# Two of four blocks of x move from the start-up into the loop's first ten steps, and wo is read in eight parts

## The chip, the core and the metric

The kernel runs on one core of a Trainium2 chip. The metric is device time in microseconds, the median of several executions. The core has five engines with a program each: PE (matrix products), DVE (vector), ACT (activations), POOL (a second vector engine) and SP, which here only issues transfers. Transfers issued by SP go through one queue; the data moves on the core's 16 DMA engines.

## The reference

One transformer block with modulated normalisation: attention of 2048 rows over a cache of 2048 keys for each of 32 heads, then a mixing layer and an MLP. Cut to what the change touches:

```python
mod = (_silu(c) @ w_mod).reshape(c.shape[0], 6, 1, -1)     # c: 640 values, w_mod: 640 x 3840
sa, ca, ga, sb, cb, gb = (mod[:, 0].copy(), ...)
h = _layernorm(x, axis=-1) * (1 + ca) + sa                 # x: 2048 x 640
q = (h @ wq).reshape(B, Sq, H, Dh)                         # 32 heads of 128
p = _softmax(einsum(q, k_cache) * Dh ** -0.5)              # per head 2048 x 2048
x = x + ga * (concat of heads(p @ v_cache) @ wo)           # wo: 4096 x 640
...                                                        # then the second half, with sb, cb, gb
```

## The kernel before

Every instruction is written by hand into one list per engine. The class `Prog` keeps those lists; `G.op` and `G.dma` append to them and derive the waits from keys that an operation reads (`r`) and writes (`w`). Each engine runs its list in order, so the order of the Python calls is the order of the work.

**Start-up (lines 380 to 483).** The 2048 rows of x come in four blocks of 512 (`load_x`), and `w_mod` in two parts: the first two of its six pieces as columns (`wmod`), the other four as rows (`wmodr`). For each block, `stats` takes means and variances on DVE (L423, L426) with the root on ACT (L428), `normed` normalises on DVE (L432, L435), and `to_hT` turns five 128-wide pieces on PE (L446) and applies scale and shift, alternating between ACT (L450) and DVE (L455). `cols` (L412) computes the scale and the shift from silu(c) on PE. `q_head0` makes the queries of head 0 for that block (`q_piece`, L294, and `q_evac`, L301). This is done for all four blocks, apart from the last block's queries, before the loop begins. `c` is read as 640 elements of two bytes by a transfer on SP's queue.

**The loop (lines 596 to 668)** has one step s for each head and each tile of 128 rows: 32 x 16 = 512 steps, and 14 more to drain. In step s PE makes the scores (`qk`, L344 and L15, two halves of 1024), DVE scales them into `negS` with a running minimum (L642, one pass for each half), POOL joins the two minima (L647), and ACT takes the exponential into a slot of `ring` (L650). `negS` holds three steps. The exponentials must be turned before they meet V. For 27 of every 32 steps that is a DMA transposition of three steps together (a trio; `transpose`, L279, on SP's queue, issued after the exponential of its last step). For the other five, PE turns them (`t_piece`, L311) and ACT copies them back (`t_evac`, L318). Ten steps later (`PVD`) PE multiplies them with V (`pv`, L358), and after every second step ACT copies the result to `Of` (L629). POOL divides by the sum and writes it to a scratch tensor in DRAM. The queries of the next head are made on the way (`q_piece` on PE, `q_evac` on ACT).

`ring` has 20 slots, given out by `take` as six windows of three (`WIN`) and two single slots (`ONE`). In the start-up the same memory holds x, `wmod`, `wmodr` and small tables; `wo` has memory of its own and is read by one transfer at the end of the start-up's issues (L393).

In steps 0 to 2 `mod_rows` (L492) multiplies silu(c) with the rows of `w_mod` on PE, spread over all partitions by `s_bc`, and ACT copies the result to `mod_bc` (L495), which the kernel first reads after the loop. The last block's queries of head 0 are made in step 0.

**SP's queue in the loop.** Besides the transpositions it holds the next head's K (`load_k`, at tile 2 of a head), the head after next's `wq` (`load_wq`, at tile 6) and the next head's V (`load_v`, at tile 11). After the loop, `a_pe` (L584) multiplies the heads' results with `wo`, and the mixing layer and the MLP follow.

## Time and profile before

| | us |
|---|---|
| median of 3 runs (1540.65 to 1544.33) | 1543.39 |
| the profiled execution | 1540.59 |
| its span, first to last instruction | 1538.4 |
| end of the last transfer of x (block 3) | 15.7 |
| first pass of DVE over scores (L642) | 35.2 |
| first exponential (L650) | 38.8 |
| exponential of step 10 | 65.4 |
| end of the last exponential, step 511 | 1222.0 |
| landing of `wo` (issued at 31.9) | 48.6 |

The page of the profile gives, for each engine, its busy time and share of the span. A line of the timeline has start, duration, engine, source line, operation, the tiles written and read and their shapes; in brackets stands how long the engine was idle before it and what released it. A line of a wait view has the engine and line that waited, what it waited for, the time in total, how often, and the longest. Where a view of one source line is narrowed to one transfer, "took" is the time that SP needed to issue it and "DMA to landing" the time from the start of the issue until its data was there.

The granted clock of PE is 0.997 over the span, and 0.90 over the first 34.5 us.

### The profile page before, as it was taken

To read this page: it belongs to the slowest core of one execution; us is meant where nothing else is said; L and a number is where in the kernel's file an instruction comes from. 1 tells how busy PE (TensorE), PEld (TensorE's weight loads), DVE (VectorE), ACT (ScalarE), POOL (GpSimd) and SP (SyncE) were. 2 spreads that over 40 slices of the span, in tenths; PEclk is the share of its full clock that TensorE was granted. 3 is DMA by queue.
4 is the path that set the end of the run, shared out by engine and by line. 5 is a ranking of instruction groups with operands and counts; after the bars stand their busy time and mean duration, and the time that the engine had idled before them with its cause. 6 is when DMAs were issued, how large, how long until landed. Compare 5 with 4: busy or idle time off the path is not lost.

```text
span 1538.4 us, 32439 instructions
## 1 busy us (share of the span) xinstructions
PE 1474.0 (96%) x13447; PEld 920.1 (60%) x12663; DVE 1372.8 (89%) x2431; ACT 1253.7 (81%) x1177; POOL 622.6 (40%) x1397
## 2 busy tenths in 40 slices
PE   5899999999999999999999999999999999999999
PEld 3366666666666666566666666666666655554545
DVE  7999999999999999999999999999999746668425
ACT  4999999999999999999999999999999800034230
POOL 0144444444444444444444444444444433323000
PEclk9999999999999999999999999999999999999999
DMA  9999999999999999999999999999999997724100
GB/s 288 239 235 238 240 246 229 255 233 248 232 248 242 247 235 233 232 245 246 238 234 244 238 232 258 229 247 239 245 236 244 236 259 165 150 63 126 35 22 35
DMA packets 1153110, 330.29 MB, mean 215 GB/s; under 512 B 1133568, under 2 KB 1146944, under 8 KB 1152960
## 3 DMA queue, kind: packets, MB, share of 16 engines
q1 hardware_dynamic: 1144480, 307.09, 100.8%
q0 software_dynamic: 6144, 16.79, 3.5%
q10 hardware_dynamic: 2336, 4.34, 0.8%
q8 instruction: 103, 1.69, 0.4%
q14 instruction: 47, 0.39, 0.1%
HBM read 43.48 MB, written 19.40 MB: 41 GB/s over the span
## 4 chain that ended last, share of the span: by engine, by line
ACT 71%; PE 20%; DVE 5%; DMA 2%; issue 1%; POOL 0%; ACTq 0%
ACT ring L650 59%; PE Sps L584 9%; ACT ring L318 5%; ACT Of L629 4%; ACT kv L301 4%; PE Sps L887 4%; DVE negS L642 3%; DMA ring<-ring 2%; PE Oaug L838 2%; PE QPp L838 2%; PE Sps L823 1%; DVE ring L423 1%; PE Oaug L760 1%; PE QPp L760 1%; DVE ring L435 0%
## 5 line engine op out<-in xcount | busy, mean ns | idle before, releaser
L642 DVE TENSOR_SCALAR_CACHE_REDUCE negS<-Sps 128x1024 f32<-128x1024 f32 x1024 | 1173.3, 1222 | 12.8 <-PE Sps L15 12.8
L650 ACT ACTIVATE ring<-negS,small 128x2048 bf16<-128x2048 f32 x512 | 1078.9, 2185 | 4.9 <-POOL small L647 4.7
L358 PEld LDWEIGHTS PTp<-kv,ring 128*128 128x128 bf16 x8192 | 557.4, 98 | 288.3 <-issue 48.5
L358 PE MATMUL PTp<-kv,ring 128*128 128x129 bf16 x8192 | 644.8, 220 | 11.9 <-DMA ring<-ring 10.9
L15 PE MATMUL Sps<-kv 128*128 128x512 bf16 x1009 | 383.1, 380 | 9.8 <-DVE negS L642 6.1
L344 PE MATMUL Sps<-kv 128*128 128x512 bf16 x956 | 370.4, 387 | 17.1 <-DVE negS L642 4.9
L647 POOL TENSOR_SCALAR small<-small 128x1 f32<-128x1 f32 x512 | 145.9, 285 | 591.3 <-DVE negS L642 591.2
L506 POOL TENSOR_SCALAR On<-Of,small 128x128 bf16<-128x128 f32 x512 | 189.8, 371 | 13.0
L344 PEld LDWEIGHTS Sps<-kv 128*128 128x128 bf16 x1024 | 98.1, 96 | 152.4 <-DVE negS L642 113.8
L629 ACT COPY Of<-PTp 128x259 f32<-128x259 f32 x256 | 139.2, 544 | 15.5 <-PE PTp L358 15.5
L499 POOL TENSOR_TENSOR small<-Of,small 128x4 f32<-128x4 f32 x128 | 133.1, 1040 | 11.8 <-ACT Of L629 11.7
L513 POOL DMA_DIRECT2D o_scratch<-On x128 | 103.4, 808 | 40.8 <-POOL On L506 37.2
L294 PE MATMUL Oaug<-hTx,kv 128*128 128x512 bf16 x258 | 97.8, 384 | 3.2 <-DVE hTx L455 3.2
L294 PE MATMUL QPp<-hTx,kv 128*128 128x512 bf16 x259 | 97.5, 381 | 2.3 <-ACT hTx L450 1.6
L768 ACT ACT_TABLE_LOAD x1 | 1.3, 1283 | 111.8 <-POOL hTx L786 111.8
L642 DVE DVE_READ_ACCUMULATOR negS<-Sps 128x1 f32 x1024 | 87.5, 85 | 0.0
L681 POOL TENSOR_SCALAR negS<-negS 128x1 f32<-128x1 f32 x48 | 24.4, 509 | 123.3 <-DVE negS L690 123.3
L584 PE MATMUL Sps<-wo,negS 128*128 128x128 bf16 (+1 forms) x503 | 69.9, 298 | 0.5
L584 PE MATMUL Sps<-wo,hTx 128*128 128x512 bf16 (+1 forms) x502 | 69.3, 297 | 0.5
L695 DVE TENSOR_TENSOR ring<-Sps,mod_bc 128x640 f32<-128x640 f32 x16 | 13.1, 821 | 60.6 <-PE Sps L584 60.6
L891 DVE TENSOR_TENSOR ring<-Sps,ring 128x640 f32<-128x640 f32 x15 | 12.4, 824 | 59.5 <-PE Sps L887 59.5
L311 PE MATMUL Oaug<-identf,ring 128*128 128x128 f32 x320 | 62.1, 276 | 1.3 <-ACT ring L650 1.3
(88 smaller groups left out, 1071.5 us busy)
## 6 DMA issues: line engine op xcount, KB each, us to landing
kv<-in_A_v_cache_dram SPq DMA_DIRECT2D x32, 512.0 KB, 5.3
o_scratch<-On POOLq DMA_DIRECT2D x128, 128.0 KB, 5.3
kv<-in_A_wq_dram SPq DMA_DIRECT2D x32, 160.0 KB, 3.4
wo<-in_A_wo_dram SPq DMA_DIRECT2D x1, 5120.0 KB, 16.7
ring<-in_A_x_dram SPq DMA_DIRECT2D x5, 640.0 KB, 6.6
ring<-in_w_mod_dram SPq DMA_DIRECT2D x1, 3200.0 KB, 14.5
out_dram<-wo SPq DMA_DIRECT2D x15, 160.0 KB, 1.7
ring<-ring SPq DMA_TRANSPOSE x144, 9.6
```

The costliest lines, as they stand in the source:

```text
L15: return t.add_instruction(mybir.InstMatmult(name=t.bass.get_next_instruction_name(), ins=[t.lower_ap(rhs), t.lower_ap(lhsT)], outs=[t.low ...
L294: G.op("tensor", lambda t: t.matmul(JB[jb], wq[:, hb, q, :], hT[:, q, cc * 512:(cc + 1) * 512], start=(q == 0), stop=(q == KT - 1)), r=[(" ...
L344: ins = (t.matmul if c2 == 0 else partial(same_weights, t))(Sps[:, col:col + 512], QT[:, hb, j * 128:(j + 1) * 128], KTs[:, hb, col:col + ...
L358: ins = t.matmul(ob[:, 0:129], pt, Vaug[:, hb, kt, 0:129], start=(kt == 0), stop=(kt == NKT - 1))
L499: G.op("gpsimd", lambda g: g.tensor_tensor(out=rl[:, 4 * b:4 * b + 4], in0=Of[:].rearrange("p a z d -> p (a z) d")[:, 4 * b:4 * b + 4, 128 ...
L506: G.op("gpsimd", lambda g: g.tensor_scalar(out=On[:, b, z, :], in0=Of[:, 2 * b + z // 2, z % 2, 0:128], scalar1=rl[:, 4 * b + z:4 * b + z ...
L513: G.dma("gpsimd", lambda e: e.dma_start(o_scr[jj // 2:jj // 2 + 2, :, hh].rearrange("a p z d -> p a (z d)"), On[:, b].rearrange("p (a z) d ...
L584: ins = t.matmul(YB[b][:, c0:c0 + cw], OTj[pr % 2][:, 2 * hh + z, :], wo[:, hh, c0:c0 + cw], start=(hh == 0), stop=(hh == H - 1))
L629: G.op("scalar", lambda a, p=p: a.copy(Of[:, p % 4].rearrange("p z d -> p (z d)")[:, 0:259], PO[:, (p % 2) * 512:(p % 2) * 512 + 259]), r= ...
L642: G.op("vector", lambda v, half=half, dst=dst, src=src, r8=r8: v.tensor_scalar(out=dst, in0=src, scalar1=-SCALE, scalar2=None, op0=ALU.mul ...
L647: G.op("gpsimd", lambda g, r8=r8: g.tensor_scalar(out=nm[:, r8:r8 + 1], in0=nm0[:, r8:r8 + 1], scalar1=nm1[:, r8:r8 + 1], scalar2=None, op ...
L650: G.op("scalar", lambda a, s=s, r8=r8: a.activation(ring[:, PSL[s], :], negS[:, s % 3, :], ACT.Exp, bias=nm[:, r8:r8 + 1], scale=-1.0), r= ...
```

## The change

The start-up does block 0 completely, and takes block 1 up to its normalised rows. The rest is written into two tables: `EARLY[s]` runs in step s after PE's work of that step, and `LATE[s]` after its exponential. Blocks 1, 2 and 3 are turned, rescaled and projected for head 0 in steps 0 to 9; the statistics of half of block 2 and all of block 3, and both normalisings, stand in steps 0 to 4, with the root on POOL in place of ACT. All rescaling of these blocks is on ACT. The five `mod_rows` move from steps 0 to 2 to steps 3 to 7 and use other banks. An exponential of one column (`dume`) in the start-up loads ACT's table before the loop.

The order of SP's issues is new: the columns of `w_mod` right after x's block 0, the first `wq` and K ahead of x's blocks 2 and 3, the rows of `w_mod` ahead of V. `c` is read as five rows of 128 on ACT's queue and turned by a matmul with `ident`. `wmod` and x lie in slots 0 to 9 of `ring`; all the other start-up buffers lie in `wo`'s memory (key `WOR`). `wo` is read in eight parts of four heads' rows (640 KB) at steps 29, 93, 157, 221, 285, 349, 413 and 461. `load_wq(2)` moves from step 6 to step 11.

```diff
-                WIN = [0, 3, 6, 11, 14, 17]
-                ONE = [9, 10]
+                WIN = [0, 3, 6, 10, 13, 16]
+                ONE = [19, 9]
...
-                free_at = dict(zip(WIN, (0, 1, 3, 2, 4, 5)))
+                free_at = dict(zip(WIN, (0, 2, 5, 4, 1, 3)))
...
+                WOP = H // 8
+
+                def load_wo(i):
+                    G.dma("sync", lambda e: e.dma_start(
+                        wo[:, i * WOP:(i + 1) * WOP], A_wo[i * WOP * 128:(i + 1) * WOP * 128, :].rearrange("(h p) n -> p h n", p=128)),
+                        ("wo", i), w=(["WOR"] if i == 0 else []) + [("wop", i)] + (["wo", "woz", "wo4"] if i == 7 else []))
+                G.dma("scalar", lambda e: e.dma_start(c_row, c[0].rearrange("(kt p) -> kt p", p=128)), "c", r=WOR, w=["c"])
                 load_x(0)
-                G.dma("sync", load_c, "c", w=["c"])
+                load_mod(0, wmod, 0, 2 * D)
                 load_x(1)
-                load_mod(0, wmod, 0, 2 * D)
+                load_wq(0)
+                load_k(0)
                 for cc in range(2, NQC):
                     load_x(cc)
-                load_wq(0)
-                load_k(0)
-                load_v(0)
-                load_mod(1, wmodr, 2 * D, 6 * D)
                 if H > 1:
                     load_wq(1)
+                load_mod(1, wmodr, 2 * D, 6 * D)
+                load_v(0)
+                if H > 1:
                     load_k(1)
-                G.dma("sync", lambda e: e.dma_start(wo[:], A_wo.rearrange("(h p) n -> p h n", p=128)), "wo", w=["wo", "woz", "wo4"])
...
+                G.op("tensor", lambda t: t.matmul(JB[0][:, 0:KT], c_row, ident[0:KT, 0:KT], start=True, stop=True),
+                     r=["c", "ident"] + WOR, w=[("J", 0)])
+                G.op("scalar", lambda a: a.activation(s_col, JB[0][:, 0:KT], ACT.Silu), r=[("J", 0)] + WOR, w=["scol"])
...
+                def root(cc, on_act):
+                    c4 = slice(4 * cc, 4 * cc + 4)
+                    if on_act:
+                        G.op("scalar", lambda a: a.activation(sd[:, c4], mv[:, c4, 1], ACT.Sqrt, bias=float(EPS)),
...
+                    else:
+                        G.op("gpsimd", lambda g: g.tensor_scalar(out=sd[:, c4], in0=mv[:, c4, 1], scalar1=float(EPS),
...
+                        G.op("gpsimd", lambda g: g.tensor_tensor(out=rstd[:, c4], in0=sd[:, c4], in1=mh4, op=ALU.pow),
...
+                def to_hT(cc, ks, banks, on_v=()):
+                    for k, b in zip(ks, banks):
+                        turn(cc, k, b)
+                    for k, b in zip(ks, banks):
+                        modul(cc, k, b, k in on_v)
...
+                stats(0, 0, 4)
+                root(0, True)
+                normed(0)
+                stats(1, 0, 2)
+                G.op("tensor", cols, r=["scol", ("wm", 0)] + WMK + WOR, w=[("J", 1)])
...
+                to_hT(0, range(KT), range(KT), (1, 3))
+                stats(1, 2, 4)
+                q_head0(0)
+                root(1, True)
+                G.op("scalar", lambda a: a.activation(dume, mh4[:, 0:1], ACT.Exp), r=["mh4"] + WOR, w=["dume"])
+                normed(1)
+                stats(2, 0, 2)
+                bcast()
+                EARLY = {0: [(to_hT, 1, (0, 1, 2), (4, 5, 7), ())],
+                         1: [(to_hT, 1, (3, 4), (4, 5), ())],
+                         2: [(to_hT, 2, (0, 1), (4, 5), ()), (q_head0, 1)],
+                         3: [(to_hT, 2, (2, 3), (4, 5), ()), (mod_rows, 0, 2)],
+                         4: [(to_hT, 2, (4,), (4,), ()), (mod_rows, 1, 1), (mod_rows, 2, 2), (q_head0, 2)],
+                         5: [(to_hT, 3, (0, 1), (4, 5), ()), (mod_rows, 3, 2)],
+                         6: [(to_hT, 3, (2, 3), (4, 5), ())],
+                         7: [(to_hT, 3, (4,), (4,), ()), (mod_rows, 4, 1)],
+                         8: [(mod_end,)],
+                         9: [(q_head0, 3)]}
+                LATE = {0: [(stats, 2, 2, 4), (root, 2, False)],
+                        1: [(normed, 2)],
+                        2: [(stats, 3, 0, 2)],
+                        3: [(stats, 3, 2, 4), (root, 3, False)],
+                        4: [(normed, 3)]}
+                WOAT = {29: [0], 93: [1], 157: [2], 221: [3], 285: [4], 349: [5], 413: [6], 461: [7]}
...
-                    G.op("tensor", f, r=[("OT", pr % 2, i) for i in parts] + [("OTa", pr % 2)] + ["wo", "woz", "wo4"], w=[("S", b)])
+                    G.op("tensor", f, r=[("OT", pr % 2, i) for i in parts] + [("OTa", pr % 2)] + ["wo", "woz", "wo4"] + [("wop", i) for i in range(8)], w=[("S", b)])
...
-                    if s <= 2:
-                        for i in ((0,), (1, 2), range(3, len(MROW)))[s]:
-                            mod_rows(i)
...
-                        if s == 0 and half == 1:
-                            q_head0(NQC - 1)
...
                     for fn, x, y in evacs:
                         fn(x, y)
+                    for fn, *args in EARLY.get(s, ()):
+                        fn(*args)
...
                         G.op("scalar", lambda a, s=s, r8=r8: a.activation(
                             ring[:, PSL[s], :], negS[:, s % 3, :], ACT.Exp, bias=nm[:, r8:r8 + 1], scale=-1.0),
                             r=[("negS", s % 3), ("nm", r8)], w=slot(PSL[s]))
+                        for fn, *args in LATE.get(s, ()):
+                            fn(*args)
                         if s in last_of:
                             transpose(last_of[s])
...
-                        if j == 6 and h + 2 < H:
+                        if j == (6 if h else 11) and h + 2 < H:
                             load_wq(h + 2)
+                        for i in WOAT.get(s, ()):
+                            load_wo(i)
```

## The prediction

> **What bounds the kernel now.** I read the page first, for the engine that the end hangs on; then the chain of waits in order of time and the timeline, for where that engine begins to be the bound; then the waits of the loop; last, single transfers on SP's queue, because the change puts more of them there.

> ```profile
> span 1538.4 us, 32439 instructions
> ...
> PE 1474.0 (96%) x13447; PEld 920.1 (60%) x12663; DVE 1372.8 (89%) x2431; ACT 1253.7 (81%) x1177; POOL 622.6 (40%) x1397
> ...
> ACT 71%; PE 20%; DVE 5%; DMA 2%; issue 1%; POOL 0%; ACTq 0%
> ACT ring L650 59%; PE Sps L584 9%; ACT ring L318 5%; ACT Of L629 4%; ACT kv L301 4%; PE Sps L887 4%; DVE negS L642 3%; DMA ring<-ring 2%; PE Oaug L838 2%; PE QPp L838 2%; PE Sps L823 1%; DVE ring L423 1%; PE Oaug L760 1%; PE QPp L760 1%; DVE ring L435 0%
> ```

> PE has the largest busy share, yet 71% of the chain lies on ACT, nearly all of it in the 512 exponentials of L650 and the copies between them. The loop is bound by ACT. In the chain an exponential takes 1.90 us from start to next start, the copy to `Of` 0.26, a projection copy (L301) 0.49, a transposed copy (L318) 0.48. For 32 steps that is 32 x 1.90 + 16 x 0.26 + 8 x 0.49 + 10 x 0.48 = 73.7 us, or 2.30 a step. Measured, from the exponential of step 10 (start 65.44) to that of step 511 (start 1220.0): 1154.6 / 501 = 2.305. DVE's two passes (L642, 1.145 from start to start) make 2.29, so it is hardly faster.

> The start-up and the first exponentials, from the timeline:

> ```profile
> 12.57 1.47 PE L412 MATMUL QPp<-ring 128*128 128x1 bf16 x50 [12.57 <-DMA ring<-in_w_mod_dram]
> ...
> 35.19 1.22 DVE L642 TENSOR_SCALAR_CACHE_REDUCE negS<-Sps 128x1024 f32<-128x1024 f32 x1 [1.85 <-PE Sps L15]
> ...
> 37.51 1.28 ACT L650 ACT_TABLE_LOAD   x1
> ...
> 38.80 2.00 ACT L650 ACTIVATE ring<-negS,small 128x2048 bf16<-128x2048 f32 x1
> ...
> 42.51 2.00 ACT L650 ACTIVATE ring<-negS,small 128x2048 bf16<-128x2048 f32 x1 [0.75 <-POOL small L647]
> ```

> The loop's first pass waits until 35.19, and steps 0 to 2 are 4.4 us apart, because the modulation rows stand on PE between them. ACT becomes the bound only at step 10:

> ```profile
> 65.44 2.00 ACT L650 ACTIVATE ring<-negS,small 128x2048 bf16<-128x2048 f32 x1 [0.29 <-POOL small L647]
> 67.35 0.36 ACT L629 COPY Of<-PTp 128x259 f32<-128x259 f32 x1
> 67.60 0.59 ACT L301 CAST kv<-Oaug 128x512 bf16<-128x512 f32 x1
> 68.08 3.94 ACT L650 ACTIVATE ring<-negS,small 128x2048 bf16<-128x2048 f32 x2
> ```

> From there ACT is never idle for long: from 65.5 to 1222 the exponentials wait 2.0 us in all. So the time is (start of exponential 10) + 501 steps at ACT's pace + a tail that the edit leaves alone.

> **The change, part by part: the start.** SP's transfers land in the order of their issue, and the gaps between landings are their prices (issue plus time to landing of each row): x block 0 at 4.9; the modulation columns 4.0 us after their forerunner (8.4 to 12.4); an x block 1.7; `wq` 0.6; the first K 2.2; the large modulation part 9.4; V 3.5; the second K 1.9. In the new order: columns 8.9, x1 10.6, `wq` 11.2, K 13.3, x2 15.0, x3 16.6, second `wq` 17.3, modulation rows 26.7, V 30.2, second K 32.1. `c` leaves this queue (five rows of 256 bytes on ACT's; a matmul against `ident` in place of the 640 two-byte pieces that land at 6.5 now). None of these is then late: V is first read at step 10, the modulation rows at step 3.

> PE's 50 column products (1.47) end at 10.4, the two copies at 10.85, 20 transposes of block 0 (2.5) at 13.0, its five rescalings (0.69 on ACT, 0.5 on DVE) at 13.85, five projection matmuls and their copy at 14.9. K is there, so the first scores do not bind; DVE does: block 0 normalised at 10.5 as now; wait for x1 to 10.6; half a block of statistics 1.83 (half of 3.24 + 0.41) to 12.4; two rescalings to 13.4; 1.83 to 15.3; root and reciprocal 0.5; normalising 1.51 to 17.3; 1.83 for half of block 2 to 19.15. The first pass of the loop starts at 19.2 in place of 35.2. ACT's table for the exponential (1.28) is loaded at 15.6 under DVE's work, not on the path.

> **The first ten steps** carry what was taken out. DVE from 19.15: 2.29 + 1.83 + 2.29 + 1.51 + 2.29 puts the end of step 2's pass at 29.4. On ACT, two rescalings of block 2 and block 1's copy to Q come first, and exponential 2 starts at 30.2. From here ACT is the bound: eight exponentials 15.2, eight rescalings 5.5, five modulation copies 2.4, three Q copies and two transposed copies 2.4: 25.5 us, so exponential 10 starts at 55.8. Added on DVE in these steps: three half statistics and two normalisings, 8.5 us; its last pass before step 10 would end at 51.9, then it waits for PE, where the projection of block 3 (step 9) waits for a transposed copy that ACT ends at 51.5, with step 10's scores queued behind it. That pass ends at 55.5, maximum ready 55.85: the cover is just used up. Gain: 65.44 - 55.8 = **9.6 us**. Bounds: 7.6 if the columns land at 12.4 as now (DVE then rescales two later); 10.5 if ACT runs from its first exponential (21.8) through all 33.1 us of work without a gap.

> The other edits cost nothing by any row: six windows of three slots and two single ones, as before, in another order; `load_wq(2)` five steps later (160 KB, 3.4 us to landing, read from step 16 on); buffers moved into `wo`. At the end `a_pe` waits for eight keys in place of one, all landed 100 us before.

> **The eight parts of `wo`.** They add no arithmetic, but stand on SP's queue at steps 29, 93, ... 413 and 461, and nothing waits for them. What waits is behind them: the transposition (L279) of steps 28 to 30, modulo 64. It already follows a V load, and is the slowest of its kind. First a usual one, then one behind a V load:

> ```profile
> L279 SPq DMA_TRANSPOSE ring<-ring x1: 6632/6632/6632, 172.3 to 172.3; - x1
> ...
> DMA to landing us min/median/max: 9.4/9.4/9.4
> ```
> ```profile
> L279 SPq DMA_TRANSPOSE ring<-ring x1: 8666/8666/8666, 262.1 to 262.1; - x1
> ...
> DMA to landing us min/median/max: 12.2/12.2/12.2
> ```

> The second (steps 92 to 94) is already late at step 102:

> ```profile
> 274.35 0.64 PE L358 MATMUL PTp<-kv,ring 128*128 128x129 bf16 x8 [0.91 <-DMA ring<-ring]
> ...
> 275.68 1.22 DVE L642 TENSOR_SCALAR_CACHE_REDUCE negS<-Sps 128x1024 f32<-128x1024 f32 x1 [0.61 <-PE Sps L15]
> ```

> PE waits 0.91, DVE 0.61, and the exponential at 277.34 starts 0.03 after its maximum is ready: the head start of DVE over ACT is gone. Any further delay there is paid by ACT in full. DVE regains 2.300 - 2.29 = 0.01 a step, 0.6 in 64 steps, and spends that on today's stalls. The whole `wo` is priced by its row:

> ```profile
> L393 SPq DMA_DIRECT2D wo<-in_A_wo_dram x1: 582/582/582, 31.9 to 31.9; - x1
> ...
> DMA to landing us min/median/max: 16.7/16.7/16.7
> ```

> It lands at 48.6, 14.7 after the second K (33.9): 1.83 us for 640 KB. A V load alone took 3.5; in the loop it lands 2.1 behind the transposition ahead of it (190.4 to 192.5) and holds back the one behind it by 12.2 - 9.4 = 2.8, so between 0.6 and 0.8 of a price arrives: 1.1 to 1.5 a part, and I take 1.3. At step 29 the transposition now lands 0.7 before its use (landing against the first L358 that reads it), and ACT has some lead: 0.4. Six more parts cost 1.3 each: 7.8. The eighth goes in behind its own trio's transposition, and the next one (step 462) has 1.8 us to spare: 0. Loss: **8.2 us**. Bounds: 0, if the transposition absorbs it; 8 x 2.4 = 19 if issue (0.58) and transfer (1.83) both arrive each time.

> [...]

> **Sum:** 1540.6 (the profiled execution; its span is 1538.4, 2.2 lie around it) - 9.6 + 8.2 = 1539.2. The runs' median, 1543.4, is 2.8 above that execution, so the forecast is 1542.0.

> **Rivals.** *The parts are hidden.* The room that a transposition has (the median over all 144 is 2.5 us from landing to first use) takes most of it: loss 0 to 3. For: only 10 DVE waits in the loop, 6.7 us, nearly all free today; against: the place of seven parts is the tightest one. Time: 1543.4 - 9.6 + 1.5 = 1535. Chance 0.36. *The parts cost more than the start gains.* Mechanism: the transposition behind each part lands later than PE's use of it, PE holds the next scores, DVE and ACT follow. It decides for slower from (9.6 + 4.6) / 8 = 1.8 us a part; at 2.4 it is 1543.4 - 9.6 + 19 = 1553. For: V's 2.8 on a smaller transfer. Against: `wo` has rows of 1280 bytes, V of 256. Chance 0.14. [...] *The start does not gain what it says*, because landings or ACT's queue in steps 2 to 9 take half of it: gain 4, loss 8.2: 1547.6. Against it stands that DVE's and ACT's sums leave only 1 us between them. Chance 0.08. *The forecast*, gain and loss within 4.6 us of each other: 0.42.

> **How the numbers follow.** Single runs of this kernel spread over 3.7 us, so 0.3% (4.6 us) is about what can be told from no change. Faster 0.36, same 0.42, slower 0.22. The forecast's own range is 1538.8 to 1548, the band itself. With the hidden case down to 10.5 us gained and nothing lost (1532.9), and the dear case up to 2.1 us a part (17 lost, 9.6 gained, 1550.8), the range is 1533 to 1551.

> **What would show it.** First pass of L642 (new L682) near 19 and exponential 10 near 56: the start is right. Seven stalls of PE's L358 (new L361) on `ring<-ring` of about 2 us near steps 38, 102, ... 422, each followed by an ACT that waits more than 1 us: the parts are right. If these waits stay under 1 us, the hidden case holds; if exponential 10 starts after 60, the start is wrong. The pace over steps 10 to 511 is 2.305 + 8.2 / 501 = 2.321 by the forecast, 2.305 if hidden, 2.343 at 2.4 a part.

## The result and the profile after

The changed kernel takes 1559.95 us in the median of six runs (1555.42 to 1566.85); the kernel before, run beside it, 1542.43 (1540.28 to 1544.33). The ratio is 1.012, with a 95% interval of 1.0092 to 1.0148: slower by 17.5 us, outside the range of 1533 to 1551 that was forecast. The profiled execution is the slowest of the six, with a span of 1565.0.

The page of the changed kernel, with the lines that answer to those shown of before:

```profile
span 1565.0 us, 32688 instructions
...
PE 1501.3 (96%) x13688; PEld 925.0 (59%) x12664; DVE 1371.0 (88%) x2423; ACT 1260.1 (81%) x1182; POOL 625.6 (40%) x1402
...
ACT 59%; PE 21%; DVE 9%; DMA 7%; issue 2%; POOL 1%; POOLq 0%; DVEq 0%; ACTq 0%
...
L682 DVE TENSOR_SCALAR_CACHE_REDUCE negS<-Sps 128x1024 f32<-128x1024 f32 x1024 | 1174.4, 1224 | 41.0 <-PE Sps L15 40.3
...
L361 PE MATMUL PTp<-kv,ring 128*128 128x129 bf16 x8192 | 651.8, 222 | 33.9 <-DMA ring<-ring 31.6
```

The same two groups on the page of the kernel before:

```profile
L642 DVE TENSOR_SCALAR_CACHE_REDUCE negS<-Sps 128x1024 f32<-128x1024 f32 x1024 | 1173.3, 1222 | 12.8 <-PE Sps L15 12.8
...
L358 PE MATMUL PTp<-kv,ring 128*128 128x129 bf16 x8192 | 644.8, 220 | 11.9 <-DMA ring<-ring 10.9
```

DVE, ACT and POOL are as busy as before; the waits have grown. In these lines the figure behind the second bar is the idle time ahead of the group, and what ended most of it: PE's products with V (L361, formerly L358) waited 31.6 us for transpositions (before: 10.9), and DVE's passes (L682, formerly L642) 40.3 us for PE's scores (before: 12.8). On the chain ACT fell from 71% to 59%, and transfers rose from 2% to 7%.

The start is where it was forecast. From the timeline of the changed kernel, the first pass over scores and the exponentials of steps 0 and 10:

```profile
19.31 1.17 DVE L682 TENSOR_SCALAR_CACHE_REDUCE negS<-Sps 128x1024 f32<-128x1024 f32 x1
...
22.49 2.00 ACT L690 ACTIVATE ring<-negS,small 128x2048 bf16<-128x2048 f32 x1
...
56.29 2.00 ACT L690 ACTIVATE ring<-negS,small 128x2048 bf16<-128x2048 f32 x1 [0.28 <-POOL small L687]
```

19.3 (forecast 19.15) and 56.3 (forecast 55.8, before 65.4). From step 10 to step 500 the pace, the mean time from one exponential's start to the next, is 2.370 us a step against 2.305. The last exponential ends at 1247.1 in place of 1222.0, and what follows it takes 317.9 us (before 316.4). So in the profiled executions the start gives 9.1 us, and the loop takes back 34.

What the loop does at the second part of `wo`, first on SP's queue and then on the engines (timeline; the bracket is the idle time before the line and what ended it):

```profile
246.78 6.61 SPq L282 DMA_TRANSPOSE ring<-ring  x1
253.44 0.58 SPq L228 DMA_DIRECT2D kv<-in_A_v_cache_dram  x1
254.06 1.38 SPq L383 DMA_DIRECT2D wo<-in_A_wo_dram  x1
255.97 11.17 SPq L282 DMA_TRANSPOSE ring<-ring  x1
```
```profile
270.36 1.05 PE L361 MATMUL PTp<-kv,ring 128*128 128x129 bf16 x8 [4.20 <-DMA ring<-ring]
...
272.73 1.23 DVE L682 TENSOR_SCALAR_CACHE_REDUCE negS<-Sps 128x1024 f32<-128x1024 f32 x1 [4.94 <-PE Sps L15]
...
274.02 0.58 ACT L321 COPY ring<-QPp 128x512 f32<-128x512 f32 x1 [4.51 <-PE QPp L314]
```

The transposition of steps 92 to 94 (the last issue) was ready at 253.7, when SP had V and then the part to issue, and so was issued 2.3 us later; its own issue then took 11.17 us (behind V alone, before: 8.67), and its data was there 14.4 us after its start, at 270.3. PE waited 4.20 for it, DVE 4.94, ACT 4.51. Before, the same step cost PE 0.91 and DVE 0.61.

To compare kernels I use one measure below, the *interval*: from the landing of the transposition of steps 25 to 27 (modulo 64) to that of steps 28 to 30, the mean of the seven places where the changed kernel has V and a part between them. It is 9.66 us before and 13.15 after: a part of 640 KB, whose bytes took 1.83 us in the whole read of the kernel before (14.7 / 8), delays what is behind it by 3.5.

### The profile page after: what moved, and what is told of

The parts are those of the page before. It is cut to its first block, busy times and chain, and to the rows that moved or that the text cites. A ratio compares the mean times of both kernels' runs of the same rounds, so it can differ in the third digit from the quotient of the medians.

```text
span 1565.0 us, 32688 instructions
## 1 busy us (share of the span) xinstructions
PE 1501.3 (96%) x13688; PEld 925.0 (59%) x12664; DVE 1371.0 (88%) x2423; ACT 1260.1 (81%) x1182; POOL 625.6 (40%) x1402
## 4 chain that ended last, share of the span: by engine, by line
ACT 59%; PE 21%; DVE 9%; DMA 7%; issue 2%; POOL 1%; POOLq 0%; DVEq 0%; ACTq 0%
ACT ring L690 49%; PE Sps L631 9%; DVE negS L682 7%; DMA ring<-ring 7%; ACT ring L321 4%; PE Sps L931 4%; ACT Of L667 3%; ACT kv L304 3%; PE Oaug L882 2%; PE QPp L882 2%; PE PTp L361 1%; PE Sps L867 1%; DMA kv<-Of 0%; ACT hTx L469 0%; PE Oaug L804 0%
## 5 line engine op out<-in xcount | busy, mean ns | idle before, releaser
L682 DVE TENSOR_SCALAR_CACHE_REDUCE negS<-Sps 128x1024 f32<-128x1024 f32 x1024 | 1174.4, 1224 | 41.0 <-PE Sps L15 40.3
L690 ACT ACTIVATE ring<-negS,small 128x2048 bf16<-128x2048 f32 x512 | 1040.7, 2070 | 11.9 <-POOL small L687 9.4
L361 PEld LDWEIGHTS PTp<-kv,ring 128*128 128x128 bf16 x8192 | 563.1, 99 | 325.7 <-issue 72.8
L361 PE MATMUL PTp<-kv,ring 128*128 128x129 bf16 x8192 | 651.8, 222 | 33.9 <-DMA ring<-ring 31.6
L347 PE MATMUL Sps<-kv 128*128 128x512 bf16 x1024 | 398.5, 389 | 9.5 <-DVE negS L682 4.4
L15 PE MATMUL Sps<-kv 128*128 128x512 bf16 x1024 | 391.1, 382 | 0.0
L547 POOL TENSOR_TENSOR small<-Of,small 128x4 f32<-128x4 f32 x128 | 133.1, 1040 | 12.8 <-ACT Of L667 12.8
L297 PE MATMUL QPp<-hTx,kv 128*128 128x512 bf16 x325 | 121.9, 382 | 1.0 <-ACT ring L321 0.9
L667 ACT COPY Of<-PTp 128x259 f32<-128x259 f32 x256 | 109.2, 427 | 16.7 <-PE PTp L361 16.6
L297 PE MATMUL Oaug<-hTx,kv 128*128 128x512 bf16 x315 | 119.2, 381 | 3.4 <-DMA kv<-in_A_wq_dram 2.2
L682 DVE DVE_READ_ACCUMULATOR negS<-Sps 128x1 f32 x1024 | 89.5, 87 | 0.0
L321 ACT COPY ring<-QPp 128x512 f32<-128x512 f32 x80 | 51.1, 639 | 20.7 <-PE QPp L314 20.5
L314 PE MATMUL QPp<-identf,ring 128*128 128x128 f32 x320 | 64.5, 285 | 0.0
```

The costliest lines, as they stand in the source:

```text
L15: return t.add_instruction(mybir.InstMatmult(name=t.bass.get_next_instruction_name(), ins=[t.lower_ap(rhs), t.lower_ap(lhsT)], outs=[t.low ...
L297: G.op("tensor", lambda t: t.matmul(JB[jb], wq[:, hb, q, :], hT[:, q, cc * 512:(cc + 1) * 512], start=(q == 0), stop=(q == KT - 1)), r=[(" ...
L321: G.op("scalar", lambda a: a.copy(dst, JB[jb]), r=[("J", jb)], w=[("PT", TSL[g], r)])
L347: ins = (t.matmul if c2 == 0 else partial(same_weights, t))(Sps[:, col:col + 512], QT[:, hb, j * 128:(j + 1) * 128], KTs[:, hb, col:col + ...
L361: ins = t.matmul(ob[:, 0:129], pt, Vaug[:, hb, kt, 0:129], start=(kt == 0), stop=(kt == NKT - 1))
L547: G.op("gpsimd", lambda g: g.tensor_tensor(out=rl[:, 4 * b:4 * b + 4], in0=Of[:].rearrange("p a z d -> p (a z) d")[:, 4 * b:4 * b + 4, 128 ...
```

## The experiments

**The halves apart.** First the start without the parts, then the parts without the start. The steps in the diffs are those of `WOAT`.

```diff
-                WOAT = {29: [0], 93: [1], 157: [2], 221: [3], 285: [4], 349: [5], 413: [6], 461: [7]}
+                WOAT = {}
...
                     load_k(1)
+                for i in (6, 7):
+                    load_wo(i)
...
-    ... OTj[pr % 2][:, 2 * hh + z, :], wo[:, hh, c0:c0 + cw],
+    ... OTj[pr % 2][:, 2 * hh + z, :], wo[:, 24 + hh % 8, c0:c0 + cw],
```

> The changed start without the parts in the loop: the last two parts of wo are read at the end of the start (their memory is free from the beginning), the other six are never read, and the output projection takes the eight heads that are there again and again (same instructions, another result). If the parts cost the loss and the start gains what its trace shows (exponential of step 10 at 56.3 us against 65.4): 1542.4 - 9.2 = about 1533 us, pace over the steps 10 to 500 about 2.305 us, and none of the long waits of DVE for scores. If something else in the change costs it (the new order of the ring's windows, the way the start leaves the queues): above 1545, with a pace of 2.34 or more.

1534.88 us (ratio to before 0.9947, 0.9934 to 0.9961), pace 2.307, the exponential of step 10 at 56.2. The new order of the windows and of the start's issues costs nothing that can be seen. This run is the base for the rest; the medians of the kernel before, run beside each of the others, lie between 1541.46 and 1542.56.

In the kernel before, the whole read of `wo` was replaced by `load_wo` at the same eight steps.

> The kernel before with wo in eight parts at the same steps as in the changed kernel, and no whole read in the start: the second half of the change alone. If the parts cost the loss, whatever the start: the changed kernel's 1560 plus the start's 9 = 1565 to 1570 us. If they cost what I forecast (8.2 us): about 1551. If they cost only together with the new start: 1540 to 1545.

1575.54 us (1.0204, 1.018 to 1.0228). The parts cost 25.1 us on the new start (1559.95 - 1534.88) and 33.2 on the old one. The interval is 13.15 in both, and from the exponential of step 10 to the end the two profiled executions take the same, 1508.8 and 1507.7 us. The time is above the 1565 to 1570 that was expected. But the changed kernel's profiled execution is its slowest and this one a middle one; where the 8 us between the medians lie was not found.

**The place.** Each part one step later, so that the first seven are issued behind the transposition of steps 28 to 30 (modulo 64); the eighth stays ahead of the transposition that it preceded:

```diff
-                WOAT = {29: [0], 93: [1], 157: [2], 221: [3], 285: [4], 349: [5], 413: [6], 461: [7]}
+                WOAT = {30: [0], 94: [1], 158: [2], 222: [3], 286: [4], 350: [5], 414: [6], 462: [7]}
```

> The changed kernel with each part one step later, so that it stands behind the transposition of the trio that ends there instead of between V and that transposition: the next transposition comes four steps later there instead of three, and nothing else stands in that gap. Theory of the place (the part and V together do not fit into the three steps between two transpositions): nearly all of the loss goes, 1533 to 1538 us. Theory of a fixed disturbance wherever a copy stands between transpositions: 1553 to 1560. Theory of the bytes alone (1.83 us a part, all on the path): 1533 + 15 = 1548.

1546.45 us (1.0024, 1.001 to 1.0037): 11.6 us over the start alone, 1.45 a part. The interval is back at 9.39; the next transposition lands 10.06 after it, in place of 6.65, and the four behind that are issued 1.4 to 3.2 us after the exponential of their last step has ended (medians; 0.0 to 0.4 in the start alone). More than half of the loss is gone, not nearly all: of the three sizes expected the one by the bytes (1548) is nearest.

The exchange of it, with the part where the change has it and V behind:

```diff
-                        if j == PVD + 1 and h + 1 < H:
+                        if j == (PVD + 4 if h % 4 == 1 else PVD + 1) and h + 1 < H:
                             load_v(h + 1)
```

> The changed kernel with the V of the heads whose V a part follows read three steps later, behind the transposition, so that V and part stand on either side of it (the exchange of the run with the parts behind: there V stayed ahead). If V and part next to each other make the excess over the bytes: the transposition behind a part lands about 9.3 us after the one ahead (7.2 to 7.6 bare and 1.83), and the time is that of the parts behind, 1543 to 1550 us. If a part of four heads has its excess wherever it stands: landing 11 us after, and 1550 to 1556.

1546.97 us (1.0033, 1.0013 to 1.0053; single runs from 1541 to 1557), interval 10.01 in the profiled execution, which is the slowest. With V on one side and the part on the other, whichever way round, the price is 1.5 a part. V and a part in the three steps between two transpositions make it 3.1.

It is not V's presence that makes the delay. With the parts behind, the transposition that follows a part is delayed by 3.4 us (10.06 against 6.65), with no V in its gap; and in the changed kernel the eighth part, whose gap holds no V either, delays its transposition (steps 462 to 464) by 3.6 (10.44 behind the landing ahead of it, against 6.81 in the start alone). What differs is the room. In the start alone the transposition of steps 32 to 34 lands 2.8 us before its first use (mean of the seven places), that of steps 28 to 30, with V ahead of it, 0.4.

**The size.** The same steps, with one head in each part, and then two, in place of four (`i * WOP + 1` or `+ 2` in place of `(i + 1) * WOP` in `load_wo`):

> The changed kernel with one head read in each part instead of four (160 KB instead of 640 KB, at the same step); the output projection takes each head that was read four times (same instructions, another result). If the loss goes with the bytes: 1533 + 27/4 = about 1540 us. If each part costs the same whatever its size: 1555 to 1560. If V alone already fills the gap and only what is beyond the slack of about 0.5 us counts: 1533 to 1536.

1535.76 us (0.9961, 0.9949 to 0.9974), interval 9.98.

> The changed kernel with two heads read in each part instead of four (320 KB, same steps); the output projection takes each head that was read twice (same instructions, another result). One head a part cost 0.9 us for eight, four heads 25. If the price is the bytes beyond a slack (0.46 us for 160 KB, 1.83 for 640 KB, and what four heads cost above that is a stall that only long waits bring): 0.92 us a part, about 0.5 beyond the slack, 1535 + 4 = 1539. If it grows evenly between the two measured points: 1535 + 9 = 1544. If a part costs its stall as soon as it is over some small size: 1553 to 1560.

1540.05 us (0.9992, 0.9981 to 1.0004), interval 10.66. Then all four heads, as four transfers one behind the other:

```diff
+                    for k in range(WOP):
+                        u = i * WOP + k
+                        G.dma("sync", lambda e, u=u: e.dma_start(wo[:, u], A_wo[u * 128:(u + 1) * 128, :]),
```

> The changed kernel with each part read by four transfers of one head, one behind the other at the same step, instead of one transfer of four heads: the same bytes at the same place. If the price of a part comes from so many bytes there (with V ahead of them): 1556 to 1564 us, and the transposition behind a part lands 13 us after the one ahead of it, as in the changed kernel. If it comes from the size of one transfer (one head alone costs 0.45 us of landing, two 1.1, four 3.6): four times 0.45, so that the landing is 11.3 us after the one ahead and the time 1535 + 8 x (1.8 - 0.45) = 1546.

1557.42 us (1.0112, 1.0083 to 1.0141), interval 12.57: the bytes at this place count, not the size of a transfer. Together:

| at the changed kernel's steps | interval | over the start alone (9.53) | time over 1534.88, a part |
|---|---|---|---|
| one head | 9.98 | 0.45 | 0.1 |
| two heads | 10.66 | 1.13 | 0.65 |
| four heads, four transfers | 12.57 | 3.04 | 2.8 |
| four heads, one transfer | 13.15 | 3.62 | 3.1 |

In every row the time is the delay less some 0.2 to 0.5 us. That is all the room that this transposition has; the rest of a delay is paid in full. And the delay grows faster than the bytes: 0.46 us of bytes delay by 0.45, 1.83 by 3.6. One transposition of each kind, from the views of that line in the runs with one head and in the changed kernel (who waited, with the time; the last line is from issue to landing, each view holds one transfer):

```profile
L282 SPq DMA_TRANSPOSE ring<-ring x1: 7342/7342/7342, 253.9 to 253.9; - x1
...
  PEld PTp L361: 0.6, 1
...
DMA to landing us min/median/max: 10.3/10.3/10.3
```
```profile
L282 SPq DMA_TRANSPOSE ring<-ring x1: 11170/11170/11170, 256.0 to 256.0; - x1
...
  PE PTp L361: 4.2, 1
...
DMA to landing us min/median/max: 14.4/14.4/14.4
```

**The queue.** The parts issued by ACT, at the same steps (`G.dma("scalar", ...)` in `load_wo`):

> The changed kernel with the parts issued by ScalarE on a queue of its own, at the same steps, instead of by SyncE between V and the transposition. If what is paid is the order in SyncE's queue (the transposition cannot begin before the part has been written out of the queue, and SyncE's own issue is late by 2 us): most of the 25 us goes, 1535 to 1542. If what is paid is the transfer engines' time, whichever queue feeds them: 1552 to 1562. ScalarE pays about 0.6 us for each issue, 5 us in all if nothing hides it.

1552.68 us (1.0076, 1.0061 to 1.009): 17.8 over the start alone, 2.2 a part. A queue of its own takes away less than a third. ACT's issues last 0.37 to 0.40 us each, 3 in all. So the larger part of the price does not hang on SP's order. The interval hides this delay: it is 9.29, as in the start alone, because here the part also delays the transposition of steps 25 to 27, which is still under way. From the landing of steps 21 to 23 to that of steps 28 to 30 it is 16.60 us in the start alone, 19.16 here and 20.16 in the changed kernel. The run with one head points the same way: the transposition of steps 28 to 30 is issued 1.9 us after the exponential of its last step has ended (0.6 in the start alone, 2.2 in the changed kernel), and yet it lands only 0.45 later behind the one ahead.

**Small pieces all over the loop.** All heads one by one, first two steps behind every V, then in the gaps of four steps that hold nothing else (with eight heads read in the start):

```diff
+                WOAT = {16 * i + 13: [i] for i in range(H)}
```

> The changed kernel with 32 transfers of one head instead of eight of four: one in every head of the loop, two steps behind the head's V as the parts were, the first at step 13. All bytes are read, at the same kind of place. If small transfers there cost what eight of them did (0.11 us each): 1535 + 3.5 = 1538 to 1539. If the slack behind V does not come back from head to head and the bytes are paid in the end: 1535 + 32 x 0.46 = 1550. If a transfer's own disturbance counts and not its bytes: over 1560.

```diff
+                WOAT = {32 * (i // 2) + (23, 30)[i % 2]: [i] for i in range(24)}
```

> The changed kernel with wo read in other pieces, all of it: the eight heads whose memory is free from the beginning at the end of the start (as in the run of the start alone), the other 24 in transfers of one head, two in every second head of the loop, each right behind the transposition after which the next comes four steps later with nothing between. If a transfer of 160 KB costs only where the slack behind it is gone (the run with one head a part: 0.9 us for eight at the worst place): 1534 to 1537 us, faster than both kernels. If every transfer costs the same wherever it is (12 us for eight parts behind the transposition, 1.45 each): 1535 + 24 x 1.45 = 1570. If the bytes have to be paid in the end (0.46 us each): 1535 + 11 = 1546.

1545.06 us (1.0019, 1.0009 to 1.0029) and 1547.53 (1.0053, 1.003 to 1.0077; single runs from 1541 to 1562). That is 10.2 us for 32 heads, 0.32 each, and 12.6 for 24, 0.53 each, against 0.46 of bytes. The first lies between what was expected by the price of single heads (1538 to 1539) and by the bytes (1550), the second near the sum by the bytes (1546). Eight single heads cost 0.1 each, but 24 or 32 are no longer free, and the empty gaps are no better than the places two steps behind V. I read this as a queue that has a little time over in the loop, which these transfers spend; no run tests that reading.

**Reading it where the queue is idle.** In the start alone the queue moves nothing from the landing of the first transposition at 41.4 to the issue of the second at 47.7. There `wo`'s memory is still taken by the rows of `w_mod`. Stored by column blocks of 512, they fill four heads' memory each, and each `mod_rows` frees one part:

```diff
-                wmodr = wof[:, 0:KT * 4 * D].rearrange("p (k n) -> p k n", k=KT)
+                wmodr = wof[:, 0:KT * 4 * D].rearrange("p (c k n) -> p c k n", k=KT, n=512)
...
-                load_mod(1, wmodr, 2 * D, 6 * D)
+                for i in range(4 * D // 512):
+                    n0 = 2 * D + 512 * i
+                    G.dma("sync", lambda e, i=i, n0=n0: e.dma_start(
+                        wmodr[:, i], w_mod[:, n0:n0 + 512].rearrange("(k p) n -> p k n", p=128)), ("wm1", i), w=[("wm1", i)])
...
+                for i in (6, 7):
+                    load_wo(i)
...
+                WOAT = {4: [0, 1], 5: [2], 6: [3], 9: [4], 13: [5]}
```

> The changed kernel with all eight parts read by step 13: the last two at the end of the start; the rows of w_mod are stored and loaded column block by column block (five transfers), so that each product of mod_rows frees the memory of one part, and parts 0 to 2 are read in the stretch from 41 to 48 us in which the queue has nothing to move, part 3 behind the transposition of steps 4 to 6, part 4 behind that of 7 to 9, part 5 behind that of 11 to 13. If what the parts cost in the loop is the queue's time and the start has time over: 1534 to 1538 us, faster than both kernels, with a pace of 2.305 to 2.31 over the steps 10 to 500. If the early trios cannot take it (slack of 11.8, 7.1, 5.3, 4.0 and 3.0 us for the first five): a loss of up to 6 x 1.83 = 11 us, 1546. If the five transfers of 1 KB rows make the start later by more than the first trio's slack: the exponential of step 10 later than 56.3 us by that amount.

1538.17 us (0.9974, 0.9965 to 0.9983), just above the best case expected (1534 to 1538): 3.3 over the start alone. Exponential 10 stands at 56.4, but behind parts 4 and 5 the transpositions of steps 14 to 39 have between 0 and 1.9 us left until their use. So these two parts were taken out, and their eight heads read one by one at the steps of the changed kernel:

```diff
+                WOAT = {4: [0, 1], 5: [2], 6: [3]}
+                WHAT = {29: 16, 93: 17, 157: 18, 221: 19, 285: 20, 349: 21, 413: 22, 461: 23}
```

> The run with everything read by step 13, but with the two parts that stood ahead of the transpositions of steps 11 to 13 and 14 to 16 (after them the trios up to step 39 had slack of 0 to 2 us) taken out of the start: their eight heads are read one by one at the eight steps of the changed kernel. If the 3.3 us that the early reading lost against the start alone came from these two parts, and a single head at those steps costs the 0.1 us that it cost before: 1534.9 + 0.9 = 1536 us, 1535 to 1537. If the first four early parts or the column blocks of w_mod lost them: 1538 to 1539, with slack near 0 again at the trio of step 14. If heads cost the 0.3 us each of the run with one in every head: 1537.5.

1536.11 us (0.9963, 0.9951 to 0.9974): 6.4 us faster than the kernel before (1542.56 beside it) and 24 faster than the changed one. It reads all of `wo`. Its page, with the lines that grew in the changed kernel:

```profile
span 1533.7 us, 32465 instructions
...
ACT 74%; PE 20%; DVE 2%; DMA 2%; issue 1%; SPq 1%; POOL 0%; DVEq 0%; ACTq 0%; POOLq 0%
...
L692 DVE TENSOR_SCALAR_CACHE_REDUCE negS<-Sps 128x1024 f32<-128x1024 f32 x1024 | 1173.7, 1214 | 10.2 <-PE Sps L15 8.8
...
L361 PE MATMUL PTp<-kv,ring 128*128 128x129 bf16 x8192 | 646.3, 221 | 13.1 <-DMA ring<-ring 9.7
```

The waits for transpositions are back at 9.7 us from 31.6, DVE's for scores at 8.8 from 40.3, and the chain lies on ACT with 74%.

## Why the prediction was wrong

**The start** was right. The first pass and exponential 10 came within 0.5 us of the forecast, and of the gain of 9.6 the start alone shows 7.4 between medians (0.39% to 0.66%, so 6 to 10 us).

**That a part delays the transposition behind it, and that PE, DVE and ACT follow,** was right, as the rival of the dear parts had it: the waits announced for steps 38, 102, ... are there, and ACT waits up to 5.85 us behind them. But the prediction's figure for a transposition's room, 2.5 us in the median, is 2.2 by the trace, and at these seven places it was 0.25 on average.

**The step that failed is the price: "between 0.6 and 0.8 of a price arrives: 1.1 to 1.5 a part, and I take 1.3".** It measures 3.1 where the change puts the part. It had two errors. The delay was taken as the 1.83 us of bytes, from a read that landed when nothing else was on the queue; in the loop it is 3.4 to 3.6, with V in the gap or without. And the share that arrives was taken from V (0.6 to 0.8), though I had myself shown that V's delay had used up the room; of a second delay 0.86 arrives (3.1 of 3.6). V's own row would have come nearer: its 2.8 us of delay for 512 KB make, by the bytes, an estimate of 3.5 for 640. That the 1.3 is near the price in the kernels with V and part on either side of a transposition (1.45 and 1.5) is luck: in the first of them a delay of 3.4 meets a room of 2.8. My upper bound, 2.4 a part for issue and transfer, was too low for the same reason.

**The small terms** went the same way. The first part, put at 0.4 because its transposition had room left, made DVE wait 1.9 us in the profiled execution. The eighth, put at nothing because it "goes in behind its own trio's transposition", made DVE wait 4.2 at 1151.5. The 1.8 us that the prediction gave to the transposition behind it are there in the kernel before; in the start alone they are 0.2.

**The pace** of 2.321 became 2.373 (2.370 to step 500), beyond the 2.343 of the dear case. Of the rivals, "the parts are hidden", which I held for almost as likely as the forecast, is refuted for 640 KB at these places and holds for eight parts of 160 KB.

**A fixed price for each transfer**, whatever its size, is not what the runs show: eight transfers of one head cost 0.9 us together, and four in place of one changed 25.1 us to 22.5. Nor is the order in SP's queue the larger share of the price: with the parts on ACT's queue 17.8 of the 25.1 us are left.

**What stays open.** Why the delay is twice the bytes: the transfers' records show it, not its cause. In the run with the parts behind, the part issued at 262.9 had no packets of V or of a transposition between its own, and its 512 packets of 1280 bytes took 55 ns each on average. The other seven of that run took 76 to 85, spread over 3.0 to 3.6 us, and those of the changed kernel 70 to 83, spread over 3.2 to 4.5. So packets are slow at a price of 1.45 as at one of 3.1, and do not tell the two apart; which resource slows them was not tried. Nor was it found why the parts alone cost 8 us more on the old start.

## What to carry to other kernels

Before a transfer is put into a loop, look at the first use of what is queued behind it: here the room there was 0.4 us, and what went beyond it was paid nearly in full at each place (3.1 us of a delay of 3.6). A price that was measured on an idle queue did not hold on the busy one here: 1.83 us became 3.4 to 3.6. If the bytes must move, first look for the stretch where the queue is idle, and free the memory they need in pieces so that they can go there; only a rest that is small against the room may go into the loop.

## What the hardware showed

PE's granted clock fell behind the long waits. The windows of the changed kernel around the wait of 4.20 us that ends at 270.36 (columns: stretch, its length, busy time of each engine, then PE's clock, the transfer engines' share, GB/s):

```profile
262.00:266.00 4.00, 4.00 (x39) 2.41 (x33) 4.00 (x9) 4.00 (x5) 1.26 (x4) 1.00 1.30 182
266.00:270.00 4.00, 0.16 (x1) 0.00 (x0) 1.79 (x4) 3.52 (x4) 1.43 (x3) 0.79 1.27 222
270.00:274.00 4.00, 3.64 (x23) 2.59 (x22) 1.23 (x2) 0.00 (x0) 0.00 (x0) 0.50 1.23 274
274.00:278.00 4.00, 4.00 (x37) 2.62 (x33) 3.04 (x5) 3.50 (x5) 2.15 (x5) 0.86 1.23 263
```

The clock is 0.50 just when PE has to catch up. From the first product after the wait to DVE's next pass it takes 2.37 us (270.36 to 272.73), while at full clock, before, it took 1.33 (274.35 to 275.68); the next pass waits another 0.91. In this execution the clock went to 0.50 after six of the eight parts, and scores ran at 0.63 us in place of 0.38 for 1 to 3 us. Behind these six DVE, with the wait of its next pass, waited 0.7 to 1.7 us longer than PE had, 7.7 in all; behind the other two it waited 0.3 less. So some 8 us of the 31 by which this execution is longer than that of the start alone may be the clock's, by this estimate. The half does not follow every long wait. In the run with V behind, 1.79 us of PE waiting was enough for 0.50; in the run on ACT's queue the clock stayed at 1.00 after 3.48:

```profile
551.00:553.00 2.00, 1.93 (x18) 1.48 (x18) 0.90 (x1) 1.52 (x2) 0.42 (x2) 0.72 1.28 279
553.00:555.00 2.00, 1.85 (x11) 1.17 (x10) 1.51 (x4) 1.58 (x2) 0.64 (x2) 0.50 1.30 309
```
```profile
709.00:712.50 3.50, 0.03 (x1) 0.03 (x2) 1.61 (x4) 3.50 (x3) 1.68 (x4) 1.00 1.22 268
712.50:714.50 2.00, 2.00 (x22) 1.21 (x20) 0.70 (x1) 0.61 (x2) 0.00 (x0) 1.00 1.33 229
```

The runs of the changed kernel spread over 11 us and those of the kernel before over 4. The two slowest of the six have mean clocks of 0.988 and 0.987, the others 0.989 to 0.991; that the clock makes this spread fits, but was not tested.
